# A sketched linear-attention and feed-forward kernel: no zero matmuls ahead of the feed-forward's first unit, and fewer, all-bf16 ones ahead of the replicated key-value sums

## The chip, the cores and the metric

The kernel runs on one core of one Trainium2 chip. The metric is the device time of one launch in microseconds (us), lower is better. A core has engines with instruction streams of their own: PE (TensorE, matmuls; PEld are its weight loads), DVE (VectorE), ACT (ScalarE), POOL (GpSimd) and SP (SyncE), which here issues nearly all DMAs. Each engine works through its stream in order and waits on semaphores for the others.

## The reference

```python
a = einsum('rd,bhsd->bhsr', S1, x); b = einsum('rd,bhsd->bhsr', S2, x)    # r = 8
phi(x) = outer product of a and b per token, 64 features
kv  = einsum('bhsf,bhsd->bhfd', phi(k), v);  z = sum over s of phi(k)
att = einsum('bhsf,bhfd->bhsd', phi(q), kv) / (phi(q) . z + 1e-6)
x   = att as (4352, 128)                       # 4 batches x 1088 tokens, 4 heads x 32
h   = x @ w_in;  g = relu(h) ** 2;  out = g @ w_out        # w_in 128 x 2048, w_out 2048 x 128
```

## The kernel before

**Tiling.** The four batches are worked through one after the other. Of each batch the keys are turned (DVE, L357), projected on the sketch (PE), multiplied to 64 features per token (`kq`, L405, POOL or DVE) and summed against the values into `KV` (PE, L561). The queries are projected, normalised (`ac`, `dn`, `rc`, `an`: L750, L760, L764, L769), multiplied to features (`qq`, L405, POOL), turned (`qu`, L795, DVE) and multiplied by the key-value sums (`X`, PE, L811); `xe` and `xr` (L973 on ACT, L974 on DVE) copy the result out of PSUM as bf16. That is the input of the feed-forward, which runs in chunks of 256 or 512 tokens and in units: `f` (first matmul, L886) fills two PSUM banks, `r` (relu) empties them into SBUF, `s` squares, `o` (second matmul, L912) accumulates, `oe` copies out and `st` stores.

Batch 0 is split in two parts: part `00` covers 256 of its query columns, part `01` the other 832. The first feed-forward chunk has 256 tokens of batch 0: its units are `f0_0` to `f0_3`, each of four matmuls 128x256.

**Order.** Nothing schedules this kernel: the string `ORDER` (L18 to L53) lists every operation, and the loop at L1081 issues them in that order to their engines. A word is name:engine:bank:dependency. Words can move between lines of the string without any effect; only their sequence counts, and for each engine only the sequence of its own words. The semaphores between engines follow from what an operation reads and writes, PSUM banks included.

**Fillers.** A word `zz:column:count:width` issues matmuls of a zero tile into PSUM that nothing reads (`fillers`, L1003). With `:w` the tile is `zero32` in fp32 (it appears in the instruction rows as `zero_70`), otherwise `zero` in bf16. Column 3584 is bank 7, column 1536 is bank 3. One fp32 matmul stands as two matmul rows in the trace.

**What stands around the change**, in the order of the string:
- `KV00` to `KV02`: key-value sums of batch 0 (L561), on PE
- `Ke0`: ACT copies them to SBUF (`kvT`, L973); `Kr0`: 16 small matmuls replicate them to the four row groups (L630); `Kv0`: ACT copies that to `kvr` (L973)
- `ci0` to `ci3`: casts of the first weight matrix, `ci0` on POOL (L974), the others on ACT (L973); `co0`, `co1`: two of the casts of the second weight matrix, on ACT
- `qq000`, `qu000`: features of the first query part (POOL, L405) and their turning (DVE, L795)
- `qp01`, `qt01`: projection of the second query part (PE, L707, into banks 0 to 3) and its turning out of PSUM (DVE, L730)
- `X000`, `xe001`, `xe000`: attention of the first part (PE, L811, banks 4 to 7) and the two copies (ACT, L973)
- `f0_0` (banks 0 and 1), `f0_1` (2 and 3), `f0_2` (4 and 5), relus `r0_0` to `r0_2` on ACT (L895)
- `ac01` to `an01` on DVE, then `kT1a`, the turning of the keys of batch 1 (DVE, L357), then `kp1` (PE, L384), `kt1` (DVE, L470), `G1` (PE, L492), `Zm1` (DVE, L961), `Wc1` (PE, L516), `X010` (PE, L811), `xe011` (DVE), `xe010` (ACT), `xr01` (DVE), `qt10` (DVE, L730), and after `G1` on PE `f0_3`, whose relu `r0_3` is on ACT

**Loads.** SP issues the loads one after the other, and each waits until a named earlier load has landed (`GATES`, L65): the halves of batch 1's queries behind `wi3` and `k1a`, the first half of its values (`v1a`) behind `k1b`, the second (`v1b`) behind `wo0`.

Of the kernel before, what the change touches and what calls it, by code (L numbers as in the profile page):

```python
# [18 lines left out]
zero LS1 ident LS2 Lk0a I16:POOL mask4 pads:POOL mask8 Lk0b Lq0p Lv0a kT0a zz:3584:1:512:w zz:3584:3:512 ST::0  # L19
Lv0b kT0b tab Lwi0 W64 qT00 Lq0r zz:3584:3:512 zz:3584:1:128 kp02::1 W3 Lwi1 kp01::2 kt02 kp00::3 kt01 SR  # L20
kq01:POOL kt00 Fq00::4 kq00 G0::5 Fe00 S2bd qp00::6 kq02:POOL Zm0 KV00::4 qt00 Lwi2:::KV00 Cp00::0 Wc0 Lwi3
ac00 KV01 W2:POOL dn00 Lk1a rc00 KV02 an00:POOL qq000:POOL Lk1b qT01 Ke0 zz:3584:1:512:w Kr0 We0 Lwo0 ci1
ci0:POOL qu000 zz:3584:1:512 qp01::0 Lwo1 Kv0 ci2 qt01 X000::4 Lq1a ac01 dn01 xe001 Lq1b xe000 ci3 rc01
zz:1536:1:512:w zz:1536:1:512 f0_0::0 an01 Lv1a kT1a f0_1::2 qq011:POOL::an01 r0_0 f0_2::4 Lv1b co0 qq012:POOL
qu011 kp1::6 r0_1 Lwo2 kt1 r0_2 qq010:POOL qu012 G1::0 s0_0:ACT kq12:POOL f0_3::2 qu010 Zm1 r0_3 qT1a Wc1
kq10:POOL Lwo3:::Wc1 X010::4 s0_3:ACT Lk2a We1 Lk2b co1 qp10::0 kq11:POOL Lq2a xe011:DVE xe010 xr01:DVE
s0_2:ACT qt10 Lq2b f2_0::4 co2:POOL f2_1::6 s0_1:ACT Lv2a r2_0:DVE f1_0::0 ac10:POOL r2_1 o0_0::2 co3:POOL
Lv2b o0_1 dn10 s2_0:ACT f1_3::4 rc10 s2_1:POOL f1_1::6 kT2a r1_0 KV10::3 KV11 r1_1 r1_3:DVE KV12 kp2::0
an10:POOL s1_0:ACT Ke1 f1_2::6 qq100:POOL Kw1 kt2 o0_2 r1_2 f2_4::4 qT2a o0_3 r2_4 qq101:POOL G2::0 qu100
f2_2::6 oe0 f2_5::4 s1_1:ACT Zm2 qq102:POOL o2_0::1 r2_2:DVE Wc2 Kd12 r2_5 f2_3::2 Kd13 We2 o2_1 qu101  # L30
s2_2:POOL r2_3 Kd11 o1_0::0 Kd10 qp20::4 qu102 s1_2:ACT f2_6::2 qt20 o1_1 kq20:POOL s2_5:ACT o2_2 o1_2
s2_3:ACT r2_6:DVE X100::4 ac20:POOL s1_3:ACT kq21:POOL dn20 f2_7::2 rc20 xe101 xr10:DVE Lk3a o1_3 xe100:DVE
an20:POOL r2_7 o2_3 Lk3b oe1:DVE f3_4::4 st0 s2_4 s2_6:ACT f3_0::6 r3_4:DVE qq200:POOL::s2_4 f3_1::2 r3_0 o2_4
Lv3a:::f3_1 o2_5 Lv3b r3_1:DVE s2_7:ACT f3_3::4 kq22:POOL o2_6 r3_3:DVE f3_5::6 s3_0:ACT f3_2::2 qq202:POOL
o2_7 r3_5 kT3a f4_1::4 KV20::0 r3_2 s3_1:POOL Lq3a KV21 r4_1:DVE Lq3b KV22 s3_3:ACT f3_6::2 st1 Ke2 f4_0::6
qu202 r3_6 o3_0::0 s3_4:POOL Kw2 o3_1 r4_0:DVE s3_2:ACT kp3::4 f4_3::2 oe2 kt3 s3_5:POOL f3_7::6 r4_3 o3_2
r3_7:DVE f4_4::4 s4_1:ACT f4_2::2 qq201:POOL G3::1 qT3a r4_2 Kd21 f4_6::6 Kd22 o3_3 r4_6 Zm3 Kd20 r4_4:DVE
f4_7::2 s4_0:POOL Kd23 Wc3 s3_6:ACT o3_4 We3 o3_5 qu200 qp30::4 r4_7 kq31:POOL qu201 o4_0::1 s3_7:ACT o3_6
qt30 o4_1 kq30:POOL s4_2:ACT f4_5::2 o3_7 r4_5:DVE s4_3:ACT X200::4 ac30:POOL kq32:POOL s4_4:ACT dn30 KV30::2
rc30 xe201 xr20:DVE xe200:DVE KV31 s4_7:ACT an30:POOL KV32 oe3:DVE f5_0::4 qq300:POOL s4_5:ACT Ke3 f5_2::6 Kw3  # L40
r5_0:DVE o4_2 st2 r5_2 f5_3::2 qq301:POOL o4_3 r5_3:DVE s5_0:ACT o4_4 f5_1::4 qq302:POOL s4_6:ACT f5_4::6
r5_1:DVE f6_4::2 o5_0::0 Kd31 r5_4 o4_5 Kd33 s5_1 f5_6::4 r6_4 Kd32 qu301 s5_2:POOL::s5_1 o4_6 Kd30 f5_7::6
r5_6 st3 qu300 o5_1 f5_5::2 r5_7 qu302 f6_0::4 s5_3:POOL o5_2 r5_5 r6_0:DVE f6_1::6 o4_7 r6_1 f6_2::2 s6_0
o5_3 r6_2 s5_7 X300::4 s5_4 s6_1:ACT oe4:DVE s5_6:POOL::s5_4 o5_4 s5_5:ACT xr30:DVE st4 xe301:DVE f6_6::2
o6_0::1 xe300:DVE s6_2:ACT o6_1 s6_4:POOL r6_6:DVE o5_5 f6_3::4 f6_5::6 r6_3:DVE f6_7::2 r6_5 o5_6 o6_2 s6_3
r6_7 f7_1::4 s6_5 o5_7 r7_1 f7_0::6 s6_7 f7_6::2 s6_6:POOL::s6_7 oe5:DVE r7_0 o6_3 r7_6:DVE o6_4 o6_5 s7_0:ACT
f7_5::4 f7_2::6 s7_1:ACT r7_5:DVE o6_6 f7_3::2 r7_2 o7_0::0 s7_6 f7_4::4 r7_3 s7_2 o7_1 f8_1::6 s7_5 r7_4
f8_4::2 s7_3 o6_7 r8_4 r8_1:DVE f7_7::4 o7_2 r7_7 f8_0::2 s7_4 o7_3 r8_0 oe6:DVE s8_1:POOL::s7_4 f8_2::6
f8_3::4 st6 r8_2:DVE s7_7:ACT o7_4 f8_5::2 r8_3 o7_5 s8_0:POOL st5 r8_5:DVE o7_6 o7_7 s8_2:ACT f8_7::4 f8_6::2
s8_3:ACT s8_5 o8_0::1 s8_4:POOL::s8_5 r8_6:DVE f9_0::6 r8_7 o8_1 o8_2 r9_0:DVE s8_7:ACT f9_1::2 o8_3 r9_1 s8_6  # L50
f9_3::4 f9_2::6 s9_0:POOL::s8_6 oe7:DVE r9_3 o8_4 r9_2:DVE st7 o8_5 s9_1:ACT o8_6 o8_7 s9_2 o9_0::0 oe8 s9_3
o9_1 st8 o9_2 o9_3 oe9 st9
"""  # L53

B, H, S, D, R = 4, 4, 1088, 32, 8
# [1068 lines left out]
```

## Time and profile before

| what | value |
|---|---|
| time, median of 3 runs | 103.64 us (103.33 to 103.7) |
| the profiled execution's own time | 104.25 us |
| its span, first to last instruction | 102.4 us |
| busy: PE, DVE, ACT, POOL | 93.5, 84.6, 85.1, 70.8 us |
| weight loads (PEld) | 64.7 us |
| filler matmuls (L1006): rows, sum, mean | 15 rows, 7.8 us, 648 ns |

Time in the trace counts from the span's start. In a row of the timeline stand the start, the length from the first start to the last end, the engine, the line, the operation, the tiles (out<-in) and the count of instructions; the bracket tells how long the engine sat idle before it and who released it. The ends of matmuls are modelled, so consecutive PE rows overlap. "Granted clock" is the TensorE clock as the records of the throttle show it, 1.00 being full speed.

### The profile page before, as it was taken

How to read it: one execution, taken by the hardware profiler on the slowest of the kernel's cores; microseconds unless marked ns; L12 is line 12 of the kernel's file. 1: busy time of each engine (PE TensorE's matmuls, PEld its weight loads, DVE VectorE, ACT ScalarE, POOL GpSimd, SP SyncE). 2: the span in 40 equal slices, each digit the busy share in tenths (PEclk: the TensorE clock that was granted, in tenths of full speed). 3: DMA queues.
4: the chain of work that ended last, by engine and by line, in shares of the span. 5: the costliest groups of instructions: out<-in, count | busy, mean ns of one | idle time of the engine just before them, and what ended most of it. 6: DMA issues, size and time to landing. Idle time of an engine off the chain costs nothing.

```text
span 102.4 us, 3821 instructions
## 1 busy us (share of the span) xinstructions
PE 93.5 (91%) x1656; PEld 64.7 (63%) x1656; DVE 84.6 (83%) x120; ACT 85.1 (83%) x101; POOL 70.8 (69%) x64
## 2 busy tenths in 40 slices
PE   5999989497899999999999998999999999999930
PEld 2267656173767766666557865776677767779930
DVE  2525669896999997999899879999999899999900
ACT  3232476999999999998999999999959999999810
POOL 5009742999899999499999999867490700976500
PEclk9999999999999999999999999999999999999998
DMA  2699799958970200766622000550040000350441
GB/s 62 217 230 302 207 297 355 244 133 244 357 159 16 58 0 16 204 171 124 193 80 55 0 6 13 127 131 8 0 107 2 0 0 6 74 134 0 102 110 51
DMA packets 10497, 11.76 MB, mean 115 GB/s; under 512 B 3056, under 2 KB 6896, under 8 KB 10480
## 3 DMA queue, kind: packets, MB, share of 16 engines
q1 hardware_dynamic: 10400, 11.51, 41.3%
q8 instruction: 13, 0.21, 1.0%
q14 instruction: 4, 0.03, 0.1%
q10 hardware_dynamic: 80, 0.01, 0.1%
HBM read 9.18 MB, written 2.33 MB: 112 GB/s over the span
## 4 chain that ended last, share of the span: by engine, by line
PE 65%; ACT 15%; DVE 10%; DMA 3%; issue 2%; SPq 0%; ACTq 0%; DVEq 0%
PE banks L886 23%; PE banks L912 19%; PE banks L1006 7%; ACT g L968 6%; ACT g L895 6%; PE banks L561 4%; DVE g L896 4%; DMA out_dram<-osb 3%; PE banks L811 3%; DVE qab L730 2%; PE banks L492 2%; PE banks L443 2%; DVE g L969 2%; ACT xT L973 2%; PE banks L707 1%
## 5 line engine op out<-in xcount | busy, mean ns | idle before, releaser
L895 ACT ACTIVATE g<-banks 128x1024 bf16<-128x1024 f32 x42 | 41.0, 1029 | 2.9 <-PE banks L886 2.6
L912 PEld LDWEIGHTS <-g 128*128 128x128 bf16 x544 | 33.5, 98 | 9.1 <-POOL g L969 0.8
L969 POOL TENSOR_TENSOR g<-g 128x1024 bf16<-128x1024 bf16 x15 | 28.2, 1894 | 13.5 <-DVE g L969 13.3
L912 PE MATMUL banks<-w_out,g 128*128 128x128 bf16 x544 | 37.2, 219 | 0.0
L968 ACT ACTIVATE g<-g 128x1024 bf16<-128x1024 bf16 x36 | 36.6, 1060 | 0.1
L886 PE MATMUL banks<-xT,w_in 128*128 128x512 bf16 (+1 forms) x144 | 34.8, 356 | 1.5 <-DVE xr L974 0.8
L896 DVE TENSOR_SCALAR g<-banks 128x1024 bf16<-128x1024 f32 x26 | 31.2, 1211 | 1.5 <-ACT g L968 0.5
L405 POOL TENSOR_TENSOR qp<-an,qab 128x768 f32<-128x768 f32 (+1 forms) x13 | 18.1, 1411 | 4.8 <-DVE an L769 3.2
L405 POOL TENSOR_TENSOR kp<-kab 128x768 f32<-128x768 f32 x11 | 16.5, 1514 | 5.3 <-ACT kab L973 5.3
L886 PEld LDWEIGHTS <-w_in 128*128 128x128 bf16 x160 | 13.6, 98 | 10.2 <-issue 4.2
L969 DVE TENSOR_TENSOR g<-g 128x1024 bf16<-128x1024 bf16 x17 | 11.7, 721 | 0.2
L795 DVE STREAM_TRANSPOSE qpT<-qp 128x768 f32<-128x768 f32 (+1 forms) x13 | 11.2, 887 | 0.6 <-POOL qp L405 0.6
L1006 PE MATMUL banks<-zero 128*128 128x512 bf16 (+2 forms) x15 | 7.8, 648 | 1.7 <-DVE zero L184 1.1
L811 PE MATMUL banks<-qpT,kvr 32*32 32x288 f32 (+4 forms) x320 | 7.1, 353 | 0.0
L357 DVE STREAM_TRANSPOSE kT<-kin 128x1088 f32<-128x1088 f32 (+1 forms) x5 | 5.4, 1070 | 2.0 <-DMA kin<-in_k_dram 2.0
L730 DVE STREAM_TRANSPOSE qab<-banks 128x1152 f32<-128x1152 f32 (+1 forms) x4 | 5.2, 1302 | 1.0 <-PE banks L707 1.0
L561 PE MATMUL banks<-kp,v 128*32 128x64 f32 (+1 forms) x288 | 5.7, 222 | 0.0
L561 PEld LDWEIGHTS banks<-kp,v 128*32 128x32 f32 (+1 forms) x288 | 4.5, 109 | 1.6 <-issue 1.1
L811 PEld LDWEIGHTS banks<-qpT,kvr 32*32 32x32 f32 x320 | 4.2, 103 | 1.3
L492 PEld LDWEIGHTS banks<-kab 128*64 128x64 f32 x72 | 2.6, 137 | 2.5 <-ACT g L895 1.6
L492 PE MATMUL banks<-kab 128*64 128x32 f32 x72 | 3.0, 224 | 1.1 <-DVE kab L470 1.1
L973 ACT COPY kab<-banks 128x192 f32<-128x192 f32 x3 | 1.0, 318 | 3.6 <-PE banks L443 3.6
(70 smaller groups left out, 67.4 us busy)
## 6 DMA issues: line engine op xcount, KB each, us to landing
kin<-in_k_dram SPq DMA_DIRECT2D x8, 272.0 KB, 3.7
out_dram<-osb SPq DMA_DIRECT2D x15, 128.0 KB, 2.5
qin<-in_q_dram SPq DMA_DIRECT2D x6, 272.0 KB, 3.7
v<-in_v_dram SPq DMA_DIRECT2D x4, 288.0 KB, 4.0
v<-in_v_dram SPq DMA_DIRECT2D x4, 256.0 KB, 4.8
qp<-in_moe_w_in_dram SPq DMA_DIRECT2D x4, 256.0 KB, 4.7
qpT<-in_moe_w_out_dram SPq DMA_DIRECT2D x4, 256.0 KB, 4.5
qin<-in_q_dram SPq DMA_DIRECT2D x1, 416.0 KB
```

The lines of the kernel that those rows point to most:

```text
L405: return eng.tensor_tensor(out=out().rearrange("p (g i j) -> p g i j", i=R, j=R), in0=a()[:, :, :, None].to_broadcast([128, n, R, R]), in1 ...
L492: ins = eng.matmul(ps(f"Z{b}")[c : c + 64, 0:32], e.kab[b][:, 64 * jj : 64 * jj + 64], k3()[:, 4 * jj : 4 * jj + 4, 0:8], start=jj < 2, st ...
L561: ins = eng.matmul(ps(f"KV{b}")[32 * h : 32 * h + 32, 0:64], e.vin[b][:P, h, jj, :], e.kp[b % 2][:P, g * 64 : g * 64 + 64], start=jj == 0, ...
L795: lambda nc, eng, ps, cols_=cols_: eng.transpose(e.qpT[b % 2][:, cols_], e.qp[b % 2][:, cols_]),
L811: ins = eng.matmul(ps(f"X{t}{i}")[32 * h : 32 * h + 32, 512 * k : 512 * k + 32 * nn], e.kvr[b][rows, 64 * h + 32 * s : 64 * h + 32 * s + 3 ...
L886: ins = eng.matmul(ps(f"H{t}")[:, u * N : (u + 1) * N], e.w_in[:, ct * 128 : ct * 128 + 128], x(), start=True, stop=True)
L895: return eng.activation(e.g[s], ps(f"H{t}"), ACTF.Relu)
L896: return eng.tensor_scalar_max(e.g[s], ps(f"H{t}"), 0.0)
L912: ins = eng.matmul(ps(f"O{ci}")[:, m * 128 : (m + 1) * 128], e.g[s][:, u * N + m * 128 : u * N + (m + 1) * 128], e.w_out[:, ct, :], start= ...
L968: return eng.activation(x, x, ACTF.Square)
L969: return eng.tensor_tensor(out=x, in0=x, in1=x, op=ALU.mult)
L1006: nc.tensor.matmul(ps[:, :cols], zero, zero[:, None, :].to_broadcast([128, cols // 128, 128]), start=True, stop=True)
```

## The change

Only the string `ORDER` is changed, and in it only filler words; all later words keep their sequence. The two fillers ahead of `f0_0` (one fp32 and one bf16 matmul, 512 columns each, into bank 3) are gone. Ahead of `Kr0`, one bf16 matmul of 512 columns and one of 256 take the place of one fp32 matmul of 512 columns, and the bf16 matmul of 512 columns that stood between `Kr0` and `qp01` is gone.

```diff
 ac00 KV01 W2:POOL dn00 Lk1a rc00 KV02 an00:POOL qq000:POOL Lk1b qT01 Ke0
-zz:3584:1:512:w Kr0 We0
+zz:3584:1:512 zz:3584:1:256 Kr0 We0
 Lwo0 ci1 ci0:POOL qu000
-zz:3584:1:512
 qp01::0 Lwo1 Kv0 ci2 qt01 X000::4 Lq1a ac01 dn01 xe001 Lq1b xe000 ci3 rc01
-zz:1536:1:512:w zz:1536:1:512
 f0_0::0 an01 Lv1a kT1a f0_1::2
```

(The lines are broken here so that the edit can be seen. The table has one line less after the change, so line numbers behind it fall by one.)

PE's stream of the kernel before, from the last key-value sums to the first weight load of the feed-forward (`zero_70` is the fp32 zero tile, `zero` the bf16 one):

```order
L561 MATMUL banks<-kp_106,v_82 32x64 x24
L1006 MATMUL banks<-zero_70 128x512
L630 MATMUL banks<-ident,kvT_98 32x128 x8
L1006 LDWEIGHTS zero
L1006 MATMUL banks<-zero 128x512
L707 MATMUL banks<-qT_80,W_73 32x224 x16
L811 MATMUL banks<-qpT_110,kvr_102 32x64 x32
L1006 MATMUL banks<-zero_70 128x512
L1006 LDWEIGHTS zero
L1006 MATMUL banks<-zero 128x512
L886 LDWEIGHTS w_in
```

The same stretch of PE's stream in the changed kernel:

```order
L560 MATMUL banks<-kp_106,v_82 32x64 x24
L1005 LDWEIGHTS zero
L1005 MATMUL banks<-zero 128x512
L1005 LDWEIGHTS zero
L1005 MATMUL banks<-zero 128x256
L629 MATMUL banks<-ident,kvT_98 32x128 x8
L706 MATMUL banks<-qT_80,W_73 32x224 x16
L810 MATMUL banks<-qpT_110,kvr_102 32x64 x32
L885 LDWEIGHTS w_in
```

Both fp32 fillers of the stretch are gone, the projection `qp01` (L706 now) stands directly behind the replication, and the feed-forward's first weight load directly behind `X000`. No row of another engine moves.

More of the change, by code (lines that the diff above doesn't have):

```diff
@@ L21 @@
 kq01:POOL kt00 Fq00::4 kq00 G0::5 Fe00 S2bd qp00::6 kq02:POOL Zm0 KV00::4 qt00 Lwi2:::KV00 Cp00::0 Wc0 Lwi3
[L22 to L50, printed above, removed]
@@ L51 @@
-f9_3::4 f9_2::6 s9_0:POOL::s8_6 oe7:DVE r9_3 o8_4 r9_2:DVE st7 o8_5 s9_1:ACT o8_6 o8_7 s9_2 o9_0::0 oe8 s9_3
-o9_1 st8 o9_2 o9_3 oe9 st9
+ac00 KV01 W2:POOL dn00 Lk1a rc00 KV02 an00:POOL qq000:POOL Lk1b qT01 Ke0 zz:3584:1:512 zz:3584:1:256 Kr0 We0
+Lwo0 ci1 ci0:POOL qu000 qp01::0 Lwo1 Kv0 ci2 qt01 X000::4 Lq1a ac01 dn01 xe001 Lq1b xe000 ci3 rc01 f0_0::0
+an01 Lv1a kT1a f0_1::2 qq011:POOL::an01 r0_0 f0_2::4 Lv1b co0 qq012:POOL qu011 kp1::6 r0_1 Lwo2 kt1 r0_2
+qq010:POOL qu012 G1::0 s0_0:ACT kq12:POOL f0_3::2 qu010 Zm1 r0_3 qT1a Wc1 kq10:POOL Lwo3:::Wc1 X010::4
@@ new lines @@
+s0_3:ACT Lk2a We1 Lk2b co1 qp10::0 kq11:POOL Lq2a xe011:DVE xe010 xr01:DVE s0_2:ACT qt10 Lq2b f2_0::4 co2:POOL
+f2_1::6 s0_1:ACT Lv2a r2_0:DVE f1_0::0 ac10:POOL r2_1 o0_0::2 co3:POOL Lv2b o0_1 dn10 s2_0:ACT f1_3::4 rc10
+s2_1:POOL f1_1::6 kT2a r1_0 KV10::3 KV11 r1_1 r1_3:DVE KV12 kp2::0 an10:POOL s1_0:ACT Ke1 f1_2::6 qq100:POOL
+Kw1 kt2 o0_2 r1_2 f2_4::4 qT2a o0_3 r2_4 qq101:POOL G2::0 qu100 f2_2::6 oe0 f2_5::4 s1_1:ACT Zm2 qq102:POOL
+o2_0::1 r2_2:DVE Wc2 Kd12 r2_5 f2_3::2 Kd13 We2 o2_1 qu101 s2_2:POOL r2_3 Kd11 o1_0::0 Kd10 qp20::4 qu102
@@ new lines @@
+s1_2:ACT f2_6::2 qt20 o1_1 kq20:POOL s2_5:ACT o2_2 o1_2 s2_3:ACT r2_6:DVE X100::4 ac20:POOL s1_3:ACT kq21:POOL
+dn20 f2_7::2 rc20 xe101 xr10:DVE Lk3a o1_3 xe100:DVE an20:POOL r2_7 o2_3 Lk3b oe1:DVE f3_4::4 st0 s2_4
+s2_6:ACT f3_0::6 r3_4:DVE qq200:POOL::s2_4 f3_1::2 r3_0 o2_4 Lv3a:::f3_1 o2_5 Lv3b r3_1:DVE s2_7:ACT f3_3::4
+kq22:POOL o2_6 r3_3:DVE f3_5::6 s3_0:ACT f3_2::2 qq202:POOL o2_7 r3_5 kT3a f4_1::4 KV20::0 r3_2 s3_1:POOL Lq3a
+KV21 r4_1:DVE Lq3b KV22 s3_3:ACT f3_6::2 st1 Ke2 f4_0::6 qu202 r3_6 o3_0::0 s3_4:POOL Kw2 o3_1 r4_0:DVE
@@ new lines @@
+s3_2:ACT kp3::4 f4_3::2 oe2 kt3 s3_5:POOL f3_7::6 r4_3 o3_2 r3_7:DVE f4_4::4 s4_1:ACT f4_2::2 qq201:POOL G3::1
+qT3a r4_2 Kd21 f4_6::6 Kd22 o3_3 r4_6 Zm3 Kd20 r4_4:DVE f4_7::2 s4_0:POOL Kd23 Wc3 s3_6:ACT o3_4 We3 o3_5
+qu200 qp30::4 r4_7 kq31:POOL qu201 o4_0::1 s3_7:ACT o3_6 qt30 o4_1 kq30:POOL s4_2:ACT f4_5::2 o3_7 r4_5:DVE
+s4_3:ACT X200::4 ac30:POOL kq32:POOL s4_4:ACT dn30 KV30::2 rc30 xe201 xr20:DVE xe200:DVE KV31 s4_7:ACT
+an30:POOL KV32 oe3:DVE f5_0::4 qq300:POOL s4_5:ACT Ke3 f5_2::6 Kw3 r5_0:DVE o4_2 st2 r5_2 f5_3::2 qq301:POOL
@@ new lines @@
+o4_3 r5_3:DVE s5_0:ACT o4_4 f5_1::4 qq302:POOL s4_6:ACT f5_4::6 r5_1:DVE f6_4::2 o5_0::0 Kd31 r5_4 o4_5 Kd33
+s5_1 f5_6::4 r6_4 Kd32 qu301 s5_2:POOL::s5_1 o4_6 Kd30 f5_7::6 r5_6 st3 qu300 o5_1 f5_5::2 r5_7 qu302 f6_0::4
+s5_3:POOL o5_2 r5_5 r6_0:DVE f6_1::6 o4_7 r6_1 f6_2::2 s6_0 o5_3 r6_2 s5_7 X300::4 s5_4 s6_1:ACT oe4:DVE
+s5_6:POOL::s5_4 o5_4 s5_5:ACT xr30:DVE st4 xe301:DVE f6_6::2 o6_0::1 xe300:DVE s6_2:ACT o6_1 s6_4:POOL
+r6_6:DVE o5_5 f6_3::4 f6_5::6 r6_3:DVE f6_7::2 r6_5 o5_6 o6_2 s6_3 r6_7 f7_1::4 s6_5 o5_7 r7_1 f7_0::6 s6_7
@@ new lines @@
+f7_6::2 s6_6:POOL::s6_7 oe5:DVE r7_0 o6_3 r7_6:DVE o6_4 o6_5 s7_0:ACT f7_5::4 f7_2::6 s7_1:ACT r7_5:DVE o6_6
+f7_3::2 r7_2 o7_0::0 s7_6 f7_4::4 r7_3 s7_2 o7_1 f8_1::6 s7_5 r7_4 f8_4::2 s7_3 o6_7 r8_4 r8_1:DVE f7_7::4
+o7_2 r7_7 f8_0::2 s7_4 o7_3 r8_0 oe6:DVE s8_1:POOL::s7_4 f8_2::6 f8_3::4 st6 r8_2:DVE s7_7:ACT o7_4 f8_5::2
+r8_3 o7_5 s8_0:POOL st5 r8_5:DVE o7_6 o7_7 s8_2:ACT f8_7::4 f8_6::2 s8_3:ACT s8_5 o8_0::1 s8_4:POOL::s8_5
+r8_6:DVE f9_0::6 r8_7 o8_1 o8_2 r9_0:DVE s8_7:ACT f9_1::2 o8_3 r9_1 s8_6 f9_3::4 f9_2::6 s9_0:POOL::s8_6
@@ L53 @@
+oe7:DVE r9_3 o8_4 r9_2:DVE st7 o8_5 s9_1:ACT o8_6 o8_7 s9_2 o9_0::0 oe8 s9_3 o9_1 st8 o9_2 o9_3 oe9 st9
 """
```

## The prediction

> **What bounds the kernel now.** The change touches one stretch, 11.5 to 17 us, so I read that stretch and what hangs on it. The page first, for the size of things:
>
> ```profile
> span 102.4 us, 3821 instructions
> ```
>
> The profiled execution took 104.25 us, 1.85 us more than its span and 0.61 us more than the median of the runs shown (103.64). I take differences in the span as differences in the time, and subtract them from the median.
>
> Next the chain that ended last, in order of time (start, length, engine, tile, line):
>
> ```profile
> 14.31 1.13 DVE qab L730
> 15.48 1.34 PE banks L1006 x3
> 16.82 0.45 PE banks L886 x4
> 17.30 1.02 ACT g L895
> ...
> 21.61 0.93 ACT g L895
> ```
>
> The fillers ahead of the first feed-forward unit stand in the chain itself: `qt01` (L730) ends, the fillers run 1.34 us, then `f0_0` and its relu. That makes them look like 1.34 us of gain. But a chain shows only what was last. What was next to last is seen engine by engine. PE in order of time:
>
> ```profile
> 11.51 1.13 PE L1006 MATMUL banks<-zero 128*128 128x512 f32 x2
> 12.57 0.64 PE L630 MATMUL banks<-ident,kvT 128*32 128x128 f32 x16
> 13.14 0.39 PE L1006 MATMUL banks<-zero 128*128 128x512 bf16 x1
> 13.46 0.66 PE L707 MATMUL banks<-qT,W 32*32 32x224 f32 x32
> 13.87 1.03 PE L811 MATMUL banks<-qpT,kvr 32*32 32x64 f32 x64
> 15.48 1.34 PE L1006 MATMUL banks<-zero 128*128 128x512 f32 x3 [0.59 <-DVE qab L730]
> 16.66 1.47 PE L886 MATMUL banks<-xT,w_in 128*128 128x256 bf16 x12
> 18.37 0.72 PE L384 MATMUL banks<-kT,W 64*32 64x288 f32 x16 [0.23 <-DVE kT L357]
> 20.19 0.74 PE L492 MATMUL banks<-kab 128*64 128x32 f32 x18 [1.10 <-DVE kab L470]
> 20.86 0.61 PE L886 MATMUL banks<-xT,w_in 128*128 128x256 bf16 x4
> ```
>
> The reader is to see two things: the fp32 filler at 11.51 holds `Kr0` (L630) back, and after `f0_0` to `f0_2` (L886) PE waits for DVE twice, for the turned keys of batch 1 and for `kt1`. Work that PE does earlier there buys nothing unless DVE is earlier too. ACT and DVE around it, in order of time:
>
> ```profile
> 11.65 0.21 ACT L973 COPY kvT<-banks 128x64 f32<-128x64 f32 x1 [1.94 <-PE banks L561]
> 11.76 1.14 ACT L973 CAST w_in<-qp 128x512 bf16<-128x512 f32 x1
> 13.28 0.37 ACT L973 COPY kvr<-banks 128x256 f32<-128x256 f32 x1 [0.38 <-PE banks L630]
> 13.55 1.23 ACT L973 CAST w_in<-qp 128x512 bf16<-128x512 f32 x1
> 14.93 0.43 ACT L973 CAST xT<-banks 128x128 bf16<-128x128 f32 x2 [0.16 <-PE banks L811]
> 15.25 1.13 ACT L973 CAST w_in<-qp 128x512 bf16<-128x512 f32 x1
> ```
>
> ```profile
> 12.04 0.15 DVE L528 TENSOR_REDUCE W<-banks 128x8 f32<-128x32 f32 x1
> 12.84 0.71 DVE L795 STREAM_TRANSPOSE qpT<-qp 128x512 f32<-128x512 f32 x1 [0.64 <-POOL qp L405]
> ...
> 16.70 0.39 DVE L769 TENSOR_TENSOR an<-qab,rec 128x224 f32<-128x224 f32 x1
> 17.01 1.30 DVE L357 STREAM_TRANSPOSE kT<-kin 128x1088 f32<-128x1088 f32 x1
> 18.28 0.71 DVE L795 STREAM_TRANSPOSE qpT<-qp 128x512 f32<-128x512 f32 x1
> 19.26 0.78 DVE L470 STREAM_TRANSPOSE kab<-banks 128x576 f32<-128x576 f32 x1 [0.27 <-PE banks L384]
> 19.97 1.53 DVE L795 STREAM_TRANSPOSE qpT<-qp 128x768 f32<-128x768 f32 x2
> 21.42 0.15 DVE L961 TENSOR_TENSOR Zm<-banks,mask 128x32 f32<-128x32 f32 x1
> ```
>
> DVE works from `qt01` at 14.31 to 21.5 with a single wait of 0.27 us, and that one follows from its own `kT1a` at 17.01. So DVE sets the pace of this stretch, and the gain is what DVE gains.
>
> **The change part by part.** *Ahead of the replication.* `Kr0` needs `kvT`, which ACT has copied at 11.65 + 0.21 = 11.86. It starts at 12.57, 0.71 later, because the fp32 filler stands before it. In its place come bf16 matmuls of 512 and 256 columns. The bf16 one of 512 at 13.14 holds the next matmul until 13.46, 0.32; half of that for 256 columns makes 0.48 together, so `Kr0` starts at 11.51 + 0.48 = 11.99, 0.58 earlier (at most 0.71, when `kvT` is there). `Kr0` keeps its pitch of 13.14 - 12.57 = 0.57. Behind it the other filler's 0.32 is gone too, so `qp01` (L707) starts at 12.56 instead of 13.46, 0.90 earlier. What it needs from DVE ended at 12.04 + 0.15 = 12.19. It ends at about 14.29 - 0.90 = 13.4.
>
> *What of it reaches DVE.* `qt01` stands on DVE behind `qu000`, which waits for POOL and ends at 12.84 + 0.71 = 13.55. So `qt01` starts at 13.57 instead of 14.31: 0.74 of the 0.90 is left. The normalising chain behind it (L750 to L769) is DVE's own, so `an01` ends at 17.09 - 0.74 = 16.35.
>
> *Ahead of the feed-forward.* `X000` (L811) needs `qu000` (13.55) and `kvr`; `Kv0` on ACT can't start before the cast ahead of it ends at 11.76 + 1.14 = 12.90 and so ends at 13.27. So `X000` starts near 13.6 instead of 13.87, and `xe000` ends near 15.15 instead of 15.36. Nothing stands between that and `f0_0` any more: banks 0 and 1 are free when `qt01` ends (13.57 + 1.12 = 14.69). `f0_0` starts near 15.2 instead of 16.66, 1.4 earlier, and its relu `r0_0` no longer waits for PE but for ACT's cast `ci3`, which then ends near 16.2: 1.1 earlier than 17.30.
>
> *What is late next.* `kT1a` would be free to start on DVE at 16.35 instead of 17.01. It needs both halves of batch 1's keys. The DMA queue shows when the second half landed, because the next load waits for exactly that:
>
> ```profile
> SPq L94 <- DMA kin<-in_k_dram: 0.7, 1, 0.7
> ```
>
> ```profile
> 16.43 1.27 SPq L94 DMA_DIRECT2D v<-in_v_dram  x2
> ```
>
> The values' load went out at 16.43 after waiting 0.7 us for the keys, so they landed just before, and no load up to here waits for anything that the change moves. `kT1a` starts at 16.43: 17.01 - 16.43 = 0.58 is left of 0.74. From here everything on DVE's line of succession moves by 0.58: `kT1a`, `kp1` on PE, `kt1` (19.26 to 18.68), `qu012` and `qu010`, `Zm1`. POOL's products, which feed the last two, follow `an01` and are 0.74 earlier, so they aren't last:
>
> ```profile
> 17.17 3.57 POOL L405 TENSOR_TENSOR qp<-an,qab 128x512 f32<-128x512 f32 x3 [3.24 <-DVE an L769]
> ```
>
> (They end at 20.74 now, 20.0 then; `qu010` would start near 20.2.) On PE, `f0_3` stands behind `G1`, which waits for `kt1`; it ends at 20.86 + 0.61 = 21.47 now and 20.89 then. ACT, 1.1 early, therefore has to wait about 0.5 us ahead of `r0_3` (21.61 in the chain): its lead shrinks to 0.58 too. The second weight matrix's first cast sits in this lead; its load had landed by 17.04, since the second half of the two loads at 16.43 waits for it, and the lead is large enough for it. From `r0_3` on no engine can be ahead by more than 0.58, every load behind it is released by work that moves along, and the streams are fixed, so the rest shifts as a block.
>
> *Sum.* 0.58 us: 103.64 - 0.58 = 103.06, which I round to 103.05 (against the profiled execution 103.67, span 101.8). The lower bound of the time is DVE's own 0.74 (when the keys land earlier), 102.9, with 0.15 for differences between executions 102.75; the upper bound, when `Kr0` gains only the 0.32 of the filler behind it and the landing is later by a quarter of a microsecond, is 0.3 of gain, 103.35.
>
> **The rivals.** *The queries of batch 1 become the late wait: no measurable change.* Behind `Zm1` DVE turns `qT1a`, now at 21.5, then at 20.9. Its second half was issued here, and its loads take so long to land (min, median, max):
>
> ```profile
> 15.42 0.33 SPq L94 DMA_DIRECT2D qin<-in_q_dram  x1
> ```
>
> ```profile
> DMA to landing us min/median/max: 3.2/3.5/5.8
> ```
>
> By the median it lands at 18.9, by the longest at 21.2, and then `qT1a` moves only 0.3: 103.35 or, with a second late landing behind it, up to 103.7. For it speaks that the DMA engines are full in this stretch, against it that only the longest would do. 0.20.
>
> *The clock falls: slower.* The fillers also keep PE busy. From 18.37 on, the least busy 3.4 us of before hold 0.72 + 0.74 + 0.61 = 2.07 us of PE work, 61%. Without fillers the first units end near 16.7, and the 3.4 us from there hold `kp1` and two thirds of `G1`, 1.2 us, 35%. What an idle PE does to the clock shows at the end (window, PE busy in the second column pair, granted clock third from the right), and what a slow clock costs at the start (weight loads of the bf16 fillers, min/median/max):
>
> ```profile
> 98.00:99.00 1.00, 0.26 (x5) 0.08 (x2) 0.00 (x0) 0.00 (x0) 0.00 (x0) 1.00 0.57 133
> 101.00:102.40 1.40, 0.00 (x0) 0.00 (x0) 0.00 (x0) 0.00 (x0) 0.00 (x0) 0.73 0.00 0
> ```
>
> ```profile
> L1006 PEld LDWEIGHTS <-zero x9: 95/151/151, 2.1 to 16.0; 128*128 128x128 bf16 x9
> ```
>
> PE ends at 98.26 and the clock falls after 101.0, so after at least 2.7 us of no work at all; slow weight loads take 151 / 95 = 1.6 times as long. If 35% counts as idle, the window after it runs slow: 2.07 us on the path (`kp1`, `G1`, `f0_3`) cost 0.6 x 2.07 = 1.2 us more, which outweighs 0.58 by 0.65: 104.3, and 105.1 if they double. It decides from the point at which 0.97 us of path work is slowed. Against it: the longest gap stays 1.1 us (from `f0_2` to `kp1`, from `kp1` to `G1`), far below 2.7. 0.13.
>
> The Trainium skill ("TensorE: Matmul & The Clock Gate", Part 1) says that PE's clock falls to half after a free-running window of about 3.4 us without activity, and that gaps over about 3 us are to be avoided. This case's end agrees (2.7 us or more). Read as gaps, the rule leaves the forecast of 103.05 standing; read as the activity in a window, it is this rival's 104.3. No run here shows yet what 35% does.
>
> *More than the sum*: an execution in which the keys land early and DVE's chain closes up, 0.8 to 1.0 of gain. 0.05.
>
> **How the numbers follow.** About 0.5% (0.52 us) is what a measurement of this kernel can tell from no change. My forecast, a gain of 0.3 to 0.75, gets 0.62; its value lies hardly above 0.52, so I give two thirds of it to faster and a third to the same. Faster 0.41 + 0.05 = 0.46; same 0.21 + 0.20 = 0.41; slower 0.13. The range 102.75 to 103.75 holds the forecast and the late queries and leaves out the clock's fall and the larger gain, 0.18 together.
>
> **What would show it.** In the changed kernel's trace: `Kr0` near 12.0, `qp01` near 12.6, `qt01` at 13.6, `f0_0` near 15.2; `kT1a` starting with the landing of the keys (near 16.4) and waiting for the DMA; ACT idle ahead of `r0_3`; and from 24 us on every row 0.58 earlier. If `kT1a` doesn't wait, DVE's 0.74 counts; if `qT1a` waits for a DMA, it is the first rival; if weight loads near 20 us take about 150 ns, the second. The prediction is wrong if the block behind 24 us doesn't shift as one.

## The result, and the profile after

The changed kernel took 104.83 us (median of 9 runs, 104.14 to 106.46), the kernel before beside it 103.64 us (9 runs, 103.06 to 104.13): ratio 1.01, interval 1.0065 to 1.0135. That is 1.2 us slower where 0.6 us faster was forecast, and above the range (102.75 to 103.75). The ratios in this document leave out runs that are over 1.5% above the fastest of their kernel, which are mostly runs in which PE's clock fell (with e11, seven of twelve runs), so a kernel that falls often loses more than its ratio says, and the table below gives the means over all runs.

The profiled execution took 104.76 us with a span of 102.8 (before: 104.25, 102.4). The two traces are thus 0.5 us apart where the medians are 1.2 apart, since the profiled execution of before was 0.6 slower than its median; why it was is not known. The changed kernel's page, the span and PE's granted clock in 40 slices of 2.57 us, in tenths:

```profile
span 102.8 us, 3814 instructions
...
PEclk9999995785999999999999999999999999999996
```

In before every slice but the last reads 9. Here four slices between 15 and 26 us are low. PE in order of time (start, length, line, tiles, idle before it), to be held against the same rows of before:

```profile
11.14 0.50 PE L1005 MATMUL banks<-zero 128*128 128x512 bf16 x2
11.57 0.64 PE L629 MATMUL banks<-ident,kvT 128*32 128x128 f32 x16
12.39 0.67 PE L706 MATMUL banks<-qT,W 32*32 32x224 f32 x32 [0.17 <-DVE W L527]
13.35 0.88 PE L810 MATMUL banks<-qpT,kvr 32*32 32x64 f32 x64 [0.29 <-ACT kvr L972]
15.59 2.64 PE L885 MATMUL banks<-xT,w_in 128*128 128x256 bf16 x12 [1.36 <-DVE rec L763]
18.16 1.15 PE L383 MATMUL banks<-kT,W 64*32 64x288 f32 x16
20.44 0.74 PE L491 MATMUL banks<-kab 128*64 128x32 f32 x18 [1.13 <-DVE kab L469]
21.11 0.61 PE L885 MATMUL banks<-xT,w_in 128*128 128x256 bf16 x4
21.88 0.41 PE L515 MATMUL banks<-Zm,S2bd 128*128 128x32 f32 x2 [0.15 <-DVE Zm L960]
22.22 1.79 PE L810 MATMUL banks<-qpT,kvr 32*32 32x224 f32 x60
```

The first units (L885) started 1.07 us earlier than in before, but took 2.64 us instead of 1.47, `kp1` (L383) 1.15 instead of 0.72, `X010` (L810 at 22.22) 1.79 instead of 1.29. (The bracket names DVE's reciprocal as what the units waited for. What they read, `xe000` on ACT, ends at 15.54, just before they start; the trace of e6 names ACT's `xT` at the same place.) DVE in the same stretch:

```profile
16.20 1.31 DVE L356 STREAM_TRANSPOSE kT<-kin 128x1088 f32<-128x1088 f32 x1 [0.18 <-DMA kin<-in_k_dram]
17.43 0.67 DVE L794 STREAM_TRANSPOSE qpT<-qp 128x512 f32<-128x512 f32 x1
19.51 0.78 DVE L469 STREAM_TRANSPOSE kab<-banks 128x576 f32<-128x576 f32 x1 [1.41 <-PE banks L383]
...
25.36 1.38 DVE L729 STREAM_TRANSPOSE qab<-banks 128x1152 f32<-128x1152 f32 x1 [0.34 <-PE banks L706]
```

The last of these rows in before:

```profile
24.68 1.37 DVE L730 STREAM_TRANSPOSE qab<-banks 128x1152 f32<-128x1152 f32 x1
```

`kT1a` is 0.81 us early (16.20 against 17.01) and waits for the keys' load, as forecast. Then DVE waits 1.41 us for PE, which it did for 0.27 us in before: `kp1` could not start before the slow units had ended, at 18.16. So `kt1` starts at 19.51, 0.25 later than in before: the 0.81 us are lost and more, at one place. The second low stretch takes `qt10` from 0.25 to 0.68 late (25.36 against 24.68), and from there the distance stays: the last matmul ends at 98.93 against 98.26, 0.67 later.

That it was the clock is in the single instructions. The twelve matmuls of the first units and their weight loads, in the changed kernel (whose first weight load, at 14.5 us, lies ahead of the stretch asked for) and then in before (min/median/max ns):

```profile
L885 PE MATMUL banks<-xT,w_in x12: 293/421/422, 15.6 to 17.8; 128*128 128x256 bf16 x12
L885 PEld LDWEIGHTS <-w_in x11: 95/152/153, 15.6 to 17.6; 128*128 128x128 bf16 x11
```

```profile
L886 PEld LDWEIGHTS <-w_in x12: 97/97/98, 16.4 to 17.8; 128*128 128x128 bf16 x12
L886 PE MATMUL banks<-xT,w_in x12: 272/272/273, 16.7 to 17.9; 128*128 128x256 bf16 x12
```

When the clock changed can be worked out from windows of 1 us. The row's third number from the right is the granted clock, a mean over the window; at half speed for a part p of the window it reads 1 - p / 2.

```profile
15.00:16.00 1.00, 0.41 (x3) 0.33 (x3) 0.93 (x3) 1.00 (x4) 0.00 (x0) 0.85 1.00 328
19.00:20.00 1.00, 0.31 (x8) 0.00 (x0) 0.49 (x1) 1.00 (x3) 0.66 (x1) 0.94 1.00 218
22.00:23.00 1.00, 1.00 (x40) 0.74 (x44) 1.00 (x2) 0.97 (x2) 1.00 (x1) 0.77 0.02 8
25.00:26.00 1.00, 1.00 (x16) 0.28 (x3) 0.66 (x2) 1.00 (x2) 0.38 (x1) 0.53 0.50 69
101.00:102.00 1.00, 0.00 (x0) 0.00 (x0) 0.00 (x0) 0.00 (x0) 0.00 (x0) 0.52 0.27 87
```

0.85 means down from 15.70; 0.94 up at 19.12; 0.77 down at 22.54; 0.53 up at 25.94; 0.52 down at 101.04. The distances are 3.42, 3.42, 3.40 and, from 25.94 to 101.04, 22 times 3.414. In this trace the clock changes only on a raster of 3.41 us. The Trainium skill ("TensorE: Matmul & The Clock Gate", Part 1) gives a free-running window of 3413 ns, and this trace agrees. So the windows between can be asked how much PE did in them (PE's busy time is the first number behind the length):

```profile
12.29:15.70 3.41, 1.66 (x97) 1.16 (x98) 3.08 (x7) 2.60 (x6) 1.21 (x2) 1.00 0.96 332
15.70:19.12 3.42, 3.42 (x28) 1.72 (x26) 2.22 (x3) 3.40 (x5) 3.03 (x3) 0.50 0.93 297
19.12:22.54 3.42, 2.13 (x64) 1.58 (x57) 3.03 (x5) 2.54 (x3) 2.70 (x3) 1.00 0.75 172
22.54:25.94 3.40, 3.40 (x98) 1.63 (x66) 1.94 (x5) 3.37 (x6) 2.84 (x3) 0.50 0.62 172
```

After a window with 1.66 us of PE work (49%) the clock halves, after a full one it is back, after one with 2.13 us (62%) it halves again. In before, the raster follows from its one change at the end (0.82 for 101 to 102 us, so 101.64), and its windows hold more:

```profile
101.00:102.00 1.00, 0.00 (x0) 0.00 (x0) 0.00 (x0) 0.00 (x0) 0.00 (x0) 0.82 0.00 0
12.90:16.31 3.41, 2.82 (x111) 1.65 (x104) 2.57 (x4) 2.87 (x5) 1.03 (x1) 1.00 0.97 310
16.31:19.73 3.42, 2.55 (x30) 1.35 (x28) 3.09 (x5) 2.50 (x5) 2.56 (x3) 1.00 0.95 300
19.73:23.14 3.41, 2.79 (x90) 2.20 (x92) 3.13 (x6) 3.38 (x5) 3.41 (x3) 1.00 0.71 156
```

Counted from the start of the span, the raster lies elsewhere in each execution (a window starts at 15.70 here and at 16.31 in before), so the same work is cut into other windows. That fits with falls in some executions of a kernel and not in others.

### The profile page after: what moved, and what is told of

Its sections match the earlier page's. It is cut to its first block, busy times and chain, and to the rows that moved or that the text cites. A ratio compares the mean times of both kernels' runs of the same rounds, so it can differ in the third digit from the quotient of the medians.

```text
span 102.8 us, 3814 instructions
## 1 busy us (share of the span) xinstructions
PE 94.0 (91%) x1652; PEld 64.7 (63%) x1652; DVE 84.8 (82%) x120; ACT 85.3 (83%) x101; POOL 70.7 (69%) x64
## 4 chain that ended last, share of the span: by engine, by line
PE 58%; DVE 14%; DMA 12%; ACT 7%; issue 3%; SPq 2%; DVEq 0%; ACTq 0%
PE banks L885 25%; PE banks L911 19%; DMA qin<-in_q_dram 5%; PE banks L810 5%; ACT g L967 4%; DVE g L895 4%; DMA out_dram<-osb 3%; DMA kin<-in_k_dram 3%; PE banks L706 3%; DVE qab L729 2%; PE banks L560 2%; PE banks L383 2%; ACT g L894 2%; DVE g L968 2%; SPq L93 2%
## 5 line engine op out<-in xcount | busy, mean ns | idle before, releaser
L885 PE MATMUL banks<-xT,w_in 128*128 128x512 bf16 (+1 forms) x144 | 36.3, 370 | 2.0 <-DVE rec L763 1.4
L885 PEld LDWEIGHTS <-w_in 128*128 128x128 bf16 x160 | 14.1, 102 | 11.5 <-issue 5.4
L810 PE MATMUL banks<-qpT,kvr 32*32 32x288 f32 (+4 forms) x320 | 7.5, 381 | 0.3 <-ACT kvr L972 0.3
L1005 PE MATMUL banks<-zero 128*128 128x512 bf16 (+3 forms) x11 | 5.1, 607 | 1.1 <-DVE zero L183 1.1
L810 PEld LDWEIGHTS banks<-qpT,kvr 32*32 32x32 f32 x320 | 4.1, 106 | 1.9 <-ACT kvr L972 0.7
L972 ACT CAST w_in<-qp 128x512 bf16<-128x512 f32 x3 | 3.4, 1124 | 1.2 <-DMA qp<-in_moe_w_in_dram 1.2
L706 PE MATMUL banks<-qT,W 32*32 32x288 f32 (+1 forms) x128 | 4.1, 467 | 0.2 <-DVE W L527 0.2
```

Source lines behind the costliest of these rows:

```text
L706: ins = eng.matmul(ps(f"qF{t}")[32 * c : 32 * c + 32, 512 * h : 512 * h + 32 * n], e.W3[r, 32 * b : 32 * b + 32], cols("q", b, r, c // 2, ...
L810: ins = eng.matmul(ps(f"X{t}{i}")[32 * h : 32 * h + 32, 512 * k : 512 * k + 32 * nn], e.kvr[b][rows, 64 * h + 32 * s : 64 * h + 32 * s + 3 ...
L885: ins = eng.matmul(ps(f"H{t}")[:, u * N : (u + 1) * N], e.w_in[:, ct * 128 : ct * 128 + 128], x(), start=True, stop=True)
```

## The experiments

**Clock theory**: what the fillers give is PE work in each window, and what the change loses is that the clock halves for a window of 3.41 us. **Landing theory**: work that starts earlier meets loads that haven't landed, and the clock is a bystander. A fall of one window takes 3.41 x 0.5 / 102 = 0.017 off a run's mean granted clock, and the idle end of the kernel takes up to 0.012 in the kept traces (e4); so a run under 0.988 is counted as one with a fall. Only one counted run, of e1 at 0.987, is near that line. Three jobs, each on one chip with its own runs of before:

| kernel | ratio (interval) | mean, all runs | runs under 0.988 | mean without / with a fall |
|---|---|---|---|---|
| before, first job | | 103.85 | 2 of 35 | 103.79 / 104.71 |
| e1 | 1.0063 (1.0016 to 1.0109) | 104.92 | 8 of 12 | 103.94 / 105.42 |
| e2 | 1.0006 (0.9957 to 1.0055) | 104.31 | 7 of 12 | 103.45 / 104.92 |
| e3 | 0.9985 (0.9938 to 1.0032) | 103.89 | 5 of 12 | 103.29 / 104.75 |
| e4 | 1.0069 (1.0032 to 1.0106) | 104.29 | 5 of 12 | 104.28 / 104.30 |
| before, second job | | 104.04 | 4 of 35 | 104.02 / 104.19 |
| e5 | 0.9946 (0.9914 to 0.9978) | 103.40 | 0 of 12 | 103.40 / none |
| e6 | 0.9954 (0.9909 to 0.9999) | 103.99 | 3 of 12 | 103.49 / 105.48 |
| e7 | 0.9969 (0.9935 to 1.0003) | 103.60 | 0 of 12 | 103.60 / none |
| e8, the changed kernel | 0.9996 (0.9944 to 1.0047) | 104.77 | 7 of 12 | 103.82 / 105.44 |
| before, third job | | 104.09 | 3 of 29 | 104.04 / 104.52 |
| e9 | 1.0031 (0.9999 to 1.0063) | 105.31 | 7 of 12 | 104.19 / 106.11 |
| e10 | 0.9952 (0.9916 to 0.9988) | 103.57 | 1 of 12 | 103.51 / 104.24 |
| e11 | 0.9896 (0.986 to 0.9933) | 104.03 | 5 of 12 | 103.30 / 105.06 |

Before falls in 9 of 99 runs; the changed kernel fell in 8 of the 9 runs of the first measurement and in 7 of 12 later.

### e1: only the fillers ahead of the first unit taken out

```diff
-zz:1536:1:512:w zz:1536:1:512 f0_0::0
+f0_0::0
```

> Half of the change alone: the replication's fillers stay as before, only the two ahead of the first unit are gone. Clock theory (PE's clock is halved for a window of 3.4 us when the window before it held too little PE work): f0_0 starts near 15.4 instead of 16.7, PE is then idle for over 1 us ahead of kp1, the clock falls in some of the runs (granted clock below 0.985 in them) and the median is 0.2 to 1.0 us above before. Landing theory (earlier work on PE, ACT and SP only meets loads that haven't landed, the clock is a bystander): the streams ahead of 15 us are as before, so nothing is lost, time within 0.3 us of before.

Mean 1.1 us above before, median 104.50, 8 of 12 runs with a fall. The streams up to `X000` are those of before, so nothing meets a load earlier there: the landing theory had it at no loss and misses. This half of the change alone is enough for a loss.

The kept trace of e1 has no fall, although one of its windows (the raster follows from the change at 103.20) holds less PE work than either window of the changed kernel that was followed by one:

```profile
14.45:17.86 3.41, 1.47 (x12) 1.10 (x12) 3.21 (x6) 2.98 (x6) 1.17 (x2) 1.00 0.93 326
17.86:21.27 3.41, 2.00 (x38) 1.15 (x38) 3.05 (x7) 2.88 (x5) 3.41 (x3) 1.00 0.94 230
103.00:104.00 1.00, 0.00 (x0) 0.00 (x0) 0.00 (x0) 0.00 (x0) 0.00 (x0) 0.60 0.00 0
```

Those 1.47 us are the twelve matmuls of the first units and nothing else. So little PE work in a window goes with falls, but PE's busy time alone doesn't decide them.

### e2: only the replication's fillers changed

```diff
-zz:3584:1:512:w Kr0 We0
+zz:3584:1:512 zz:3584:1:256 Kr0 We0
...
-zz:3584:1:512 qp01::0
+qp01::0
```

> The other half alone: fewer and bf16 fillers ahead of the replication, the two ahead of the first unit stay. Clock theory: the fillers ahead of the unit keep the windows from 12 to 20 us busy, no fall or few (granted clock over 0.985), and of the 0.58 us of gain forecast some 0.3 to 0.6 is there: 0.3 to 0.6 us below before. Landing theory: what starts early is qp01 and all behind it, which is what meets the late loads, so the loss of the whole change, 0.5 to 1.2 us above before, is here.

Both miss. The clock theory expected few falls and found them in 7 of 12; the landing theory expected the whole loss, and the runs without a fall are 0.34 us below before. So this half gives something and makes falls too, and over all runs its mean is 0.46 us above before: the loss isn't e1's half alone. In its trace, which has no fall, DVE waits for the queries:

```profile
22.29 1.31 DVE L357 STREAM_TRANSPOSE qT<-qin 128x1088 f32<-128x1088 f32 x1 [1.44 <-DMA qin<-in_q_dram]
```

That is the first rival of the prediction (the late queries), at 1.44 us. How much of the gain it takes, no run shows by itself.

### e3: the changed kernel with fillers where PE waits anyway

```diff
-f0_0::0
+zz:1536:4:512 f0_0::0
```

> The changed kernel with four bf16 matmuls of 512 columns put into bank 3 ahead of f0_0, where PE waits for ACT anyway (14.4 to 15.3 us in the trace of after). Clock theory: the fall near 15.7 goes in most runs, PE's first units take 1.5 us instead of 2.6, and the time is below the changed kernel by 0.5 to 1.5 us; a fall near 22.5 may remain. Landing theory: no load lands earlier for it, time as the changed kernel, 104.8 within 0.3.

The mean is 103.89, 0.05 above before beside it, where the changed kernel lay 1.5 (first measurement) and 0.7 us (e8) above before: about 1 us is back for four matmuls that nothing reads. 5 of 12 runs still fall. The trace has one of them, on its raster:

```profile
12.34:15.75 3.41, 2.90 (x118) 1.64 (x107) 2.74 (x6) 2.67 (x6) 1.67 (x2) 1.00 0.75 212
15.75:19.17 3.42, 1.89 (x29) 1.14 (x26) 2.45 (x4) 3.33 (x4) 2.76 (x3) 1.00 0.98 346
19.17:22.58 3.41, 2.15 (x64) 1.58 (x57) 3.06 (x5) 2.92 (x4) 3.00 (x3) 1.00 1.02 240
22.58:25.99 3.41, 3.41 (x97) 1.62 (x66) 2.00 (x5) 3.38 (x6) 2.81 (x3) 0.50 0.72 208
```

The filled window (2.90 us) is followed by no fall, the one with `G1` and `Wc1` (2.15 us) by one, as expected. But the window from 15.75, with only 1.89 us, is not: it holds ten of the wide matmuls of the first units beside `kp1`, the other the small ones of the Gram sum and of `X010`. PE's busy time alone doesn't sort them, as in e1.

### e4: a wait in the place of the fillers

```diff
-zz:1536:1:512:w zz:1536:1:512 f0_0::0
+f0_0::0:rc01
```

> The kernel before with its two fillers ahead of f0_0 taken out and f0_0 made to wait for the reciprocal of the second query part on DVE (rc01, 16.3 to 16.7 us), so that the unit starts when it starts in before but PE does nothing in the 1.3 us of the fillers. Clock theory: PE's work, not the time, is what the fillers give, so the clock falls in part of the runs and the time is 0.3 to 1.5 us above before. Landing theory, and any theory by which the fillers matter through when the unit starts: as before within 0.3 us.

Slower by 0.7%, as the clock theory had it, with 5 of 12 runs with a fall. But here runs with and without a fall take the same time (104.30, 104.28), and those without lie 0.49 us above the runs of before without one. So the loss of this kernel isn't shown to come from the falls. The wait also sat at the unit's last matmul, so three of its matmuls ran early. e9 mends that.

### e5: the changed kernel with all three gaps filled

```diff
-f0_0::0
+zz:1536:4:512 f0_0::0
...
-kp1::6
+zz:3584:2:512 kp1::6
...
-G1::0
+zz:512:4:512 G1::0
```

> The changed kernel with bf16 fillers in the three places where PE waits anyway: four ahead of f0_0 (bank 3), two ahead of kp1 (bank 7), four ahead of G1 (bank 1). Clock theory: hardly a run falls (granted clock over 0.988 in at least 10 of 12, against 1 of 9 of the changed kernel), and what is left is the earlier start: 0.3 to 0.6 us below before, near 103.3. Landing theory: the fillers change no landing, time as the changed kernel, near 104.8.

No run of 12 falls, and the kernel is faster than both: 103.39 us median, 0.9946 (0.9914 to 0.9978) of before. The windows of its trace hold 3.17, 2.58 and 2.69 us where those of the changed kernel held 1.66 and 2.13:

```profile
13.67:17.09 3.42, 3.17 (x81) 2.38 (x82) 2.63 (x7) 2.76 (x5) 1.02 (x2) 1.00 0.96 321
17.09:20.50 3.41, 2.58 (x35) 0.89 (x33) 3.05 (x4) 3.36 (x5) 3.28 (x4) 1.00 0.96 278
20.50:23.91 3.41, 2.69 (x84) 1.74 (x80) 2.58 (x6) 2.91 (x4) 3.41 (x3) 1.00 0.93 202
```

The landing theory had it at 104.8 and misses: the waits for the loads are still in this trace (0.65 us ahead of `kT1a`, 0.83 ahead of `qT1a`), and the kernel is 1.4 us faster in the mean than the changed one beside it (e8). Of that, 0.94 us is what the changed kernel's mean (104.77) lies above its own runs without a fall (103.82); the other 0.42 is not the clock by this count.

### e6: only the gap ahead of G1 filled

```diff
-G1::0
+zz:512:4:512 G1::0
```

> The changed kernel with the four fillers ahead of G1 alone. Clock theory: the second fall (near 22.5 us in the trace of after) goes, the first (near 15.7) stays where the windows lie so; at most one fall a run (granted clock hardly under 0.975), mean time between e5 and the changed kernel, 103.8 to 104.5. Landing theory: as the changed kernel.

3 of 12 runs fall, mean 103.99, between e5 and the changed kernel, as expected; one run (0.967) has more than the one fall that was foreseen. The kept trace has no fall, so which of the two falls the fillers prevent isn't shown.

### e7: before with the same gap filled

The edit of e6, made to the kernel before.

> The kernel before with four fillers added ahead of G1. Clock theory: before falls in 2 of 35 runs only, so there is little to win, and the fillers stand in a wait of 1.1 us: as before within 0.3 us. A theory by which fillers in this gap speed things up by themselves (so that e5 and e6 would win without any fall being avoided): 0.3 us or more below before.

The ratio's interval (0.9935 to 1.0003) takes in no change, but the mean is 0.44 us below before, 0.42 with the runs without a fall alone, more than the 0.3 that the clock theory allowed. In its trace the stretch isn't quicker: from `kp1` to the first `o` matmuls (L912) it takes 18.84 to 26.95, 8.11 us, against 8.17 in before. Where the gain comes from stays open. It is as large as the 0.42 us by which e5 lies below the changed kernel's runs without a fall, and e5 has the same fillers, so not all of e5's gain can be put down to the earlier start and the clock.

### e8: the changed kernel again

No edit.

> The changed kernel once more, beside the others on one chip. Clock theory: two runs of three or more show a granted clock under 0.988; runs with one fall are about 1 us and those with two about 2 us slower than runs with none, and runs with none lie at or below before's 103.75. Landing theory: the time does not go with the granted clock.

7 of 12 with a fall; 103.82 without, 105.03 with one (2 runs), 105.60 with more (5 runs). The time goes with the clock, and without a fall the changed kernel is 0.2 us below before. In its trace the keys land late (`kT1a` at 17.20 after waiting 1.20 us), which leaves 1.20 us of PE work in a window; the next one, at half speed, holds 2.48 us and is followed by another slow one, so that two in a row are slow:

```profile
16.06:19.47 3.41, 1.20 (x21) 0.37 (x18) 1.91 (x3) 2.59 (x4) 3.39 (x3) 1.00 0.86 279
19.47:22.88 3.41, 2.48 (x35) 2.20 (x43) 3.36 (x5) 1.94 (x3) 2.72 (x3) 0.50 0.82 213
22.88:26.30 3.42, 3.42 (x97) 1.85 (x98) 1.23 (x5) 3.39 (x5) 2.44 (x3) 0.50 0.65 182
```

### e9: the whole unit waits in the place of the fillers

The edit of e4, with the wait ahead of the unit's first weight load:

```diff
-zz:1536:1:512:w zz:1536:1:512 f0_0::0
+f0_0::0:rc01
...
-                return ins
+                    first = ins if u == 0 else first
+                return first
```

> As e4 (no fillers ahead of f0_0, the unit waits for rc01 on DVE), but now the wait stands ahead of the unit's first weight load instead of its last matmul, so that PE does nothing from the end of X000 to the start of the unit, which starts when it starts in before. Clock theory: windows without work are commoner than in before (2 and 4 of 35 runs), at least 4 of 12 runs show a granted clock under 0.988, mean 0.3 to 1.2 us above before. Any theory by which only the time of the start matters: within 0.3 us of before.

Mean 105.31, 1.2 us above before; 7 of 12 runs with a fall, 106.11 against 104.19 for those without, which are 0.15 above before's. The unit starts when DVE's reciprocal is there, as late as behind the fillers, and PE is empty ahead of it:

```profile
16.48 1.47 PE L886 MATMUL banks<-xT,w_in 128*128 128x256 bf16 x12 [1.92 <-DVE rec L764]
```

That empty time costs what the fillers were there to save. So it is the work in the gap that counts here, not when the unit starts.

### e10: e5 without the replication's fillers

```diff
-zz:3584:1:512 zz:3584:1:256 Kr0 We0
+Kr0 We0
```

> e5 without the two bf16 fillers ahead of Kr0, which then waits for kvT alone. Clock theory: 0.1 us is freed ahead of qp01 that DVE can't use (qt01 waits for qu000), and the window before 15 us holds 0.5 us less work: as e5 within 0.3 us, a few runs with a fall (0 to 3 of 12). A theory by which the fillers ahead of the replication matter through the replication's start: 0.1 to 0.4 us below e5.

As e5 within the noise (103.57 against 103.40 in the mean, 1 fall): in its trace `Kr0` starts 0.34 us after the end of the sums, in e5 0.36, since it waits for `kvT` anyway.

### e11: e5 with half of its fillers

```diff
-zz:1536:4:512 f0_0::0
+zz:1536:2:512 f0_0::0
...
-zz:3584:2:512 kp1::6
+zz:3584:1:512 kp1::6
...
-zz:512:4:512 G1::0
+zz:512:2:512 G1::0
```

> e5 with half of its fillers (two ahead of f0_0, one ahead of kp1, two ahead of G1). Clock theory with a threshold of PE work in a window: falls come back in part of the runs, 1 to 5 of 12 with a granted clock under 0.988, mean 0 to 0.6 us above e5. A theory by which any matmul in a gap is enough: no run with a fall, as e5.

5 of 12 runs fall, mean 104.03 against 103.57 for e10 in the same job. So it is a matter of how much work: any matmul in a gap isn't enough. Its trace has two slow windows in a row, as e8's:

```profile
16.39:19.81 3.42, 1.68 (x21) 0.34 (x19) 2.71 (x4) 3.13 (x5) 3.38 (x3) 1.00 0.91 287
19.81:23.22 3.41, 3.38 (x57) 2.75 (x58) 3.00 (x5) 1.96 (x3) 3.36 (x3) 0.50 0.61 157
23.22:26.63 3.41, 3.19 (x75) 1.60 (x66) 1.72 (x3) 3.41 (x5) 1.64 (x2) 0.50 0.80 242
```

## Why the prediction was wrong

**The steps up to DVE held.** Measured against forecast: `qp01` 12.39 (12.56), `qt01` 13.23 (13.57), `kT1a` 16.20 (16.43), and that one bound by the keys' landing, which was named as what is late next. Part of the lead came from this execution itself, whose key-value sums ended 0.37 us earlier: counted from their end, `qt01` starts after 2.02 us where 1.99 was forecast. `f0_0` was 0.4 late (15.59 against 15.2), because ACT's cast `ci2` waited for its weights until 14.11; that step was missed. The prediction had the unit off DVE's line, and at full speed it would be; in this trace the slow units held up `kp1` and so DVE.

**The sum of 0.58 us was about right for an execution that keeps its clock.** Over the seven kernels that have the replication's change (e10 goes further and takes out all of its fillers), the 56 runs without a fall lie 0.53 us below the runs of before without one, job by job. That number is not a clean measurement of the earlier start, since runs without a fall are a choice among runs, e7 gained 0.42 without it, and the changed kernel's own five in e8 gained 0.20.

**The step that failed** is that the sum has no term for PE's clock. The clock was set aside as a rival with a chance of 0.13, in the words that "the longest gap stays 1.1 us ... far below 2.7". That is a reading of gaps, and gaps were the wrong quantity. The 2.7 us came from the end of before (PE done at 98.26, clock down after 101.0), which is one cut of a raster: in the changed kernel the end falls at 101.04 after PE's last matmul at 98.93, 2.1 us. In the middle it falls with no idle stretch over 1.36 us, after windows with 49% and 62% of PE work, and 8 of 9 runs had a fall.

The rival's mechanism was right, and so was looking at how much PE does in 3.4 us. The window that it named, with 1.2 us of work (35%) behind the first units, is not one of the two in the changed kernel's first trace; it is in e8's (1.20 us from 16.06), and a fall follows. Its slowing by 1.6 held (421 against 272 ns for a matmul, 1.55), and its price of 1.2 us for one slow window, before the gain is taken off, is near the 1.21 us of e8's two runs with one fall. What it left out is that a run can have more than one: e8's five such runs lie 1.78 us above those without, and over all experiments the 48 runs with one or more falls lie 1.45 us above the runs without one of the same kernels. That the block behind 24 us shifts as one held, with the other sign.

**The queries' rival** is there too (waits of 0.83 us in e5, 1.44 in e2). Both of these traces are without a fall, and no run separates what such a wait costs.

**Left open**: what exactly the window counts (1.47 us in e1 and 1.89 in e3, mostly wide matmuls, kept the clock; 1.66, 2.13 and 2.15 us with many narrow ones did not); why e7 gained; why e4 is slower in runs without a fall too; and the spread of before's own runs without a fall (102.74 to 105.25), for which no experiment was made.

## What to carry to other kernels

Matmuls of zeros that nothing reads can be load-bearing: before taking one out, add up PE's work in each stretch of 3.4 us around it, not only the idle gaps, and don't let it drop below what the kernel holds today. The sum is a warning and no more: windows with as little as 1.47 us kept the clock here and others with 2.15 us did not. Put such fillers where PE waits anyway (a bank that is free, a wait that something else sets); e5 has ten of them there and is 0.64 us faster in the mean than before. A cost that strikes in some executions and not in others shows in the granted clock of each run before it shows in one profile.

## What the runs showed of the hardware that was not expected

- The clock needs far less than an idle window to fall: 1.20 to 2.15 us of PE work in 3.41 us were followed by half speed (e8, the changed kernel, e11, e3, e4). Windows at full speed with 2.19 us (e9), 2.39 (before) and more were followed by none; from 1.47 (e1) to 2.15 it went both ways.
- It doesn't always come back after one window: half-speed windows with 2.48 us (e8) and 3.38 us (e11) of PE work were followed by another slow one, windows with 3.19 us (e11, the next) and 3.42 us (e8) by full speed. Busy time doesn't sort these either.
- The column of the granted clock reads 1.00 in the first microseconds of every trace here, while the weight loads of the first bf16 fillers take 146 to 153 ns, as at a clock of 0.50 (152 ns), and not 97. So it isn't to be trusted ahead of the first change that it shows.
